# Batch 1's inputs laid out like batch 0's, and the head of an attention–MoE kernel in another order

## The chip, the cores and the metric

The kernel runs on one core of a Trainium2 chip. The metric is the device time of one execution in microseconds. The kernel before takes 725.71 us, the median of three runs (725.63 to 726.22).

## What is computed

Two batched attentions between tokens `x` and a small state share one score matrix. Their outputs, joined along the sequence, run through two mixture layers of the same shape, each a dense pair of matrices around a nonlinearity.

```python
# x: B, H, S, D = 4, 8, 512, 64; state: 4, 8, 32, 64
scores = x @ state.T / sqrt(D);  a  = softmax(scores);  xread = a  @ state
scores2 = state @ x.T / sqrt(D); a2 = softmax(scores2); sread = a2 @ x
x = concat([xread, sread], axis=2)         # 4*544 = 2176 rows of 512 after the transpose
h = x @ w_in                               # 512 -> 2048
g = where(h >= 1, h, where(h <= -1, 0, (h + 1)**2 / 4))
x = g @ w_out                              # 2048 -> 512
h = x @ w_in2; g = max(h, 0) + log1p(exp(-abs(h))); out = g @ w_out2
```

## The kernel before, in words

**Numbers.** Inputs come as 64-bit words and are read as pairs of 32-bit words. A weight tile is rebuilt by three steps of the class `Pair`: `scale` (ScalarE, L124) on the high words, `tail` (VectorE, L143) shifts the low words, and `join` (VectorE, L146) puts the two together. Products that need full accuracy are made of three, from a high part `hi` (ScalarE copy, L85) and a low part `lo` (VectorE subtraction, L88) of each factor: high by high, high by low, low by high (L623 to L625, L683).

**First layer without the read.** For a batch, `G = state · W_in` is computed once per pair of column tiles (`g_mm` by `heads`, L287), so the first layer of its tokens is the softmax weights `a` times `G`: six products at L683 for each hidden tile. A hidden tile goes through its activation (L772, L773 on ScalarE, L788 on VectorE), is cut into `gth` (ScalarE, L85) and `gtl` (VectorE, L88), and enters the second layer (L623 to L625).

**Order.** All is written out by hand: the kernel runs in `tc.manual_schedule()`, so each engine's queue holds its instructions in program order. A head (from `st0 = load_state0(...)` on) prepares batch 0; then a loop over windows runs. Window `i` carries the steps that a list of `ORDER` names: `l1` (first layer of this window's tile), `l2` (second layer of an earlier one), `hi`, `lo`, `open`, `close` (cuts and activations), `early`, `conv`, `split`, `load` (weights), `pe`, `copy` (other work). `when(i, kind, fn)` hangs work on a window. `HW` and `TW` hold windows for attention steps, and `HW[0]` that of `place_state`, which turns the state of all batches (TensorE L274, VectorE copy L275).

**The head.** `load_state0` brings the state of batch 0, 64 partitions, on ScalarE's queue; `load_x(0)` brings `x` of batch 0 in two loads of 1 KB runs on SyncE's queue, and `load_x(1)` that of batch 1 in four loads of 256-byte runs, behind the loads of the first weight pair. `warm` issues dummy products of the identity (L219). `x_transpose` turns `x` (L320 for batch 0, L316 for batch 1), `x_copy` moves the result to SBUF (ScalarE L85, the fourth VectorE L327); `place_state0` turns the state (TensorE L235, VectorE L236 into `stT0`). `scores_n` (L249) makes 64 narrow score products, `f_sub` and `f_exp` start the softmax, `scores0` (L261) makes the scores of the other side. `f_norm` sums, inverts and multiplies one half of the weights, with VectorE and GpSimd sharing it (L531 to L534); `f_turn` (L540) turns them for `n_hi` and `n_lo`, which cut them into `ahi` and `alo`. `x_turn` and `x_keep` turn `x` of batch 1 and keep it. Banks of PSUM are named `at` (with two halves `side`), `l1`, and `acc0` to `acc3`.

Of the kernel before, what the change touches and what calls it, by code (L numbers as in the profile page):

```python
# [18 lines left out]
def fused_kernel(ctx: ExitStack, tc: tile.TileContext, x, state, w1, w2, w3, w4, out):  # L19
# [79 lines left out]
    class Pair:  # L99
# [41 lines left out]

        def tail(self, d, raw):
            nc.vector.tensor_scalar(d, raw[:, 0::2], 29, None, op0=ALU.logical_shift_right)  # L143
# [28 lines left out]

    ident = new(p1, [P, P], F32, "ident")
    make_identity(nc, ident)
    stT = new(p1, [P, NJ, B * N], F32, "stT")
    stT0 = new(p1, [P, H * N], F32, "stT0")
# [3 lines left out]

    xt = {}

    def load_x(b, engs):
# [3 lines left out]
        if b == 0:  # L187
# [33 lines left out]
    def load_state0(eng):  # L221

        st = new(base, [P, 1024], F32, "cv", 2)[: H * N // 4]
        eng.dma_start(st[:, : 4 * D], state[0].rearrange("h (m i) d -> (h m) (i d)", i=4))
        return st

    def place_state0(st):

        n = H * N // 4
        one = st[:, : 4 * D].rearrange("p (i d) -> p i d", i=4)  # L230
        two = st[:, 512:].rearrange("p (i q d) -> p i q d", i=4, q=2)
        nc.vector.tensor_copy(two, one.unsqueeze(2).to_broadcast([n, 4, 2, D]))
        ps = at_bank()[:, : H * N]
        for i in range(4):
            nc.tensor.transpose(ps[:, i * n : (i + 1) * n], two[:, i].rearrange("p q d -> p (q d)"), ident[:n, :n])  # L235
        nc.vector.tensor_copy(stT0.rearrange("p (m i) -> p m i", i=4), ps.rearrange("p (i m) -> p m i", i=4))  # L236

    def scores_n(xT, js, out):


        for j in js:
            for e in range(2):
                for i in range(2):
                    for q in range(2):
# [5 lines left out]
                            out[q][:, o : o + N], xT[j][rows, c : c + P], stT0[rows, h * N : (h + 1) * N], start=True, stop=True  # L250
                        )

    def scores0(xT):

        for j in range(NJ):
            for e in range(2):
                for q in range(2):
# [4 lines left out]
                        side[j * N : (j + 1) * N, q, c], stT0[rows, h * N : (h + 1) * N], xT[j][rows, c], start=True, stop=True  # L262
# [14 lines left out]
    def heads(b, o, rhs):  # L277


        for j in range(NJ):  # L280
            for e in range(2):
                rows = slice(e * D, (e + 1) * D)
                if b == 0:
                    s_h = stT0[rows, (2 * j + e) * N : (2 * j + e + 1) * N]
                else:
                    s_h = stT[rows, j, b * N : (b + 1) * N]
# [15 lines left out]
    class Attn:  # L302
# [10 lines left out]
        def x_transpose(self, j, ps, r):  # L313
            xb, c = xt[self.b], slice(r * P, (r + 1) * P)
            if self.b > 0:
# [13 lines left out]
        def scores(self):  # L329

            if self.b == 0:
                scores0(self.xT)
            else:
                heads(self.b, lambda e: side[:, e, :], lambda j: self.xT[j])
            if self.b == 0:
                self.ps.update((g, side.rearrange("p q (e i t) -> p e q i t", e=2, i=2)[:, g]) for g in range(NG))
            else:
                self.ps.update((g, side[:, g, :]) for g in range(NG))
# [5 lines left out]
        def turned(self, t):  # L344

            return t.rearrange("p (i q t) -> p q i t", i=2, q=2) if self.b == 0 else t
# [114 lines left out]
        def x_turn(self):  # L461
            for j in range(NJ):
# [4 lines left out]
        def x_keep(self, i):  # L467

            t = new(p1, [P, NG, S], F32, ("ahi", "alo")[i])
            for e in range(2):  # L470
                j = 2 * i + e
                self.xT[j] = t[:, e, :]
                copy(self.xT[j], self.ps["x", j])
# [53 lines left out]
        def f_norm(self, J, eng):  # L527
            h = self.f_half(self.f, J)
            sm = new(at, [P, 2 * NB], F32, "sm", 2)[:, :NB]
            sm3 = sm.rearrange("p (c j) -> p c j", j=2)  # L530
            nc.vector.tensor_reduce(sm3, h, axis=AX.X, op=ALU.add)  # L531
            nc.vector.tensor_scalar(sm, sm, 1e-9, None, op0=ALU.add)
            nc.vector.reciprocal(sm, sm)
            eng.tensor_tensor(h, h, sm3.unsqueeze(3).to_broadcast([P, NB // 2, 2, N]), op=ALU.mult)  # L534
# [293 lines left out]
    HW = [5, 0, 6, 15, 17]  # L828
# [23 lines left out]
    for n, (a, pair) in enumerate(pairs):  # L852
# [73 lines left out]
    when(1, "pe", lambda: warm(W_[2]))  # L926
    when(1, "copy", lambda: [a0.s_copy(g) for g in range(NG)])
# [27 lines left out]
    with tc.manual_schedule():  # L955
# [11 lines left out]
        for J in range(2):  # L967
# [3 lines left out]
            if J == 0:  # L971
                place_state0(st0)
# [105 lines left out]
```

## Time and profile before

| what | value |
|---|---|
| median of 3 runs | 725.71 us (725.63 to 726.22) |
| the profiled execution's own time | 727.52 us |
| its span | 725.7 us |
| TensorE busy | 713.9 us (98%), 4038 instructions |
| VectorE busy | 443.1 us (61%) |
| ScalarE busy | 444.0 us (61%) |
| GpSimd busy | 17.9 us (2%) |
| mean granted clock of TensorE | 0.995 |

The span reaches from the first to the last instruction of one profiled execution; 1.8 us of that execution lie outside it, and it took 1.8 us more than the median run. Busy shares are means over stages with different limits, so a row of a stage counts for more than these. All times below are microseconds from the span's start.

### The profile page before, as it was taken

How to read it: one execution, taken by the hardware profiler on the slowest of the kernel's cores; microseconds unless marked ns; L12 is line 12 of the kernel's file. 1: busy time of each engine (PE TensorE's matmuls, PEld its weight loads, DVE VectorE, ACT ScalarE, POOL GpSimd, SP SyncE). 2: the span in 40 equal slices, each digit the busy share in tenths (PEclk: the TensorE clock that was granted, in tenths of full speed). 3: DMA queues.
4: the chain of work that ended last, by engine and by line, in shares of the span. 5: the costliest groups of instructions: out<-in, count | busy, mean ns of one | idle time of the engine just before them, and what ended most of it. 6: DMA issues, size and time to landing. Idle time of an engine off the chain costs nothing.

```text
span 725.7 us, 10250 instructions
## 1 busy us (share of the span) xinstructions
PE 713.9 (98%) x4038; PEld 577.9 (80%) x4038; DVE 443.1 (61%) x699; ACT 444.0 (61%) x730; POOL 17.9 (2%) x22
## 2 busy tenths in 40 slices
PE   8899999999999999999999999999999999999997
PEld 7667777777777887778888888888888888888886
DVE  5789975574684245767798756544555545544543
ACT  4787775555654356677887766555566556565553
POOL 0001200021000000000000000000000000000000
PEclk8999999999999999999999999999999999999999
DMA  9993005326150013353443011020002100010001
GB/s 264 387 291 120 0 1 118 60 64 112 59 172 4 1 62 114 131 172 118 146 145 131 22 38 59 11 63 0 1 0 79 39 0 1 1 58 1 1 0 58
DMA packets 61951, 56.29 MB, mean 78 GB/s; under 512 B 40976, under 2 KB 42832, under 8 KB 61904
## 3 DMA queue, kind: packets, MB, share of 16 engines
q1 hardware_dynamic: 61680, 55.46, 24.3%
q8 instruction: 31, 0.51, 0.3%
q10 hardware_dynamic: 224, 0.20, 0.1%
q14 instruction: 16, 0.13, 0.1%
HBM read 45.68 MB, written 9.96 MB: 77 GB/s over the span
## 4 chain that ended last, share of the span: by engine, by line
PE 89%; DMA 3%; DVE 3%; ACT 2%; SPq 2%; issue 1%; DVEq 0%; ACTq 0%
PE acc L623 16%; PE acc L624 16%; PE acc L625 16%; PE l L683 10%; PE l L624 9%; PE l L625 9%; PE l L623 9%; PE at L287 2%; PE l L670 2%; DMA wq<-in_moe_w_out_dram 1%; SPq L196 1%; DMA wq<-in_moe_w_in_dram 1%; DMA xs<-in_state_dram 1%; DVE cv L146 1%; PE at L413 1%
## 5 line engine op out<-in xcount | busy, mean ns | idle before, releaser
L88 DVE TENSOR_TENSOR gtl<-tl,gth 128x512 fp32r<-128x512 f32 x64 | 44.3, 692 | 144.1 <-ACT gth L85 143.9
L781 ACT ACTIVATE ta<-l 128x512 f32<-128x512 f32 x68 | 40.7, 598 | 132.3 <-PE l L625 132.3
L624 PE MATMUL acc<-gtl,wq 128*128 128x512 f32 x256 | 100.1, 391 | 2.0 <-DVE gtl L88 2.0
L623 PE MATMUL acc<-gth,wq 128*128 128x512 f32 x256 | 101.2, 395 | 0.6 <-ACT gth L85 0.6
L625 PE MATMUL acc<-gth,wq 128*128 128x512 f32 x256 | 99.7, 390 | 0.0
L88 DVE TENSOR_TENSOR gtl<-ta,gth 128x512 fp32r<-128x512 f32 x68 | 47.3, 696 | 67.1 <-ACT gth L85 67.1
L772 ACT ACTIVATE ta<-l 128x512 f32<-128x512 f32 x68 | 40.3, 593 | 47.3 <-PE l L683 31.1
L623 PE MATMUL acc<-wq,gth 128*128 128x512 f32 x152 | 59.2, 390 | 0.0
L624 PE MATMUL acc<-wq,gth 128*128 128x512 f32 x152 | 59.2, 389 | 0.0
L625 PE MATMUL acc<-wq,gtl 128*128 128x512 f32 x152 | 59.2, 389 | 0.0
L623 PEld LDWEIGHTS acc<-gth,wq 128*128 128x128 f32 x256 | 48.0, 188 | 13.3 <-issue 1.7
L624 PEld LDWEIGHTS acc<-gtl,wq 128*128 128x128 f32 x256 | 48.1, 188 | 12.8 <-DVE gtl L88 3.2
L625 PEld LDWEIGHTS acc<-gth,wq 128*128 128x128 f32 x256 | 48.1, 188 | 10.2
L623 PE MATMUL acc<-wh,gth 128*128 128x512 f32 x136 | 52.9, 389 | 0.0
L624 PE MATMUL acc<-wl,gth 128*128 128x512 f32 x136 | 52.9, 389 | 0.0
L625 PE MATMUL acc<-wh,gtl 128*128 128x512 f32 x136 | 52.9, 389 | 0.0
L88 DVE TENSOR_TENSOR tl<-tl,ta 128x512 f32<-128x512 f32 x68 | 47.0, 692 | 2.4
L788 DVE SCALAR_TENSOR_TENSOR ta<-ta,l 128x512 f32<-128x512 f32 x68 | 46.2, 679 | 0.5 <-ACT ta L773 0.5
L791 DVE SCALAR_TENSOR_TENSOR tl<-l,tl 128x512 f32<-128x512 f32 x68 | 46.5, 684 | 0.0
L792 DVE SCALAR_TENSOR_TENSOR ta<-tb,ta 128x512 f32<-128x512 f32 x68 | 46.4, 682 | 0.0
L85 ACT ACTIVATE gth<-ta 128x512 fp32r<-128x512 f32 x68 | 42.1, 619 | 6.8 <-DVE ta L788 6.8
L784 ACT ACTIVATE tl<-tb 128x512 f32<-128x512 f32 x68 | 43.0, 633 | 2.2
(189 smaller groups left out, 1475.5 us busy)
## 6 DMA issues: line engine op xcount, KB each, us to landing
ws<-in_moe_w_in_dram SPq DMA_DIRECT2D x20, 512.0 KB, 4.7
ws<-in_moe_w_out_dram SPq DMA_DIRECT2D x20, 512.0 KB, 4.1
wq<-in_moe_w_in_dram SPq DMA_DIRECT2D x12, 512.0 KB, 7.1
wq<-in_moe_w_out_dram SPq DMA_DIRECT2D x12, 512.0 KB, 8.8
xd<-xs SPq DMA_DIRECT2D x16, 256.0 KB, 3.0
xs<-xd SPq DMA_DIRECT2D x16, 256.0 KB, 3.9
out_dram<-xs SPq DMA_DIRECT2D x15, 256.0 KB, 2.3
x<-in_x_dram SPq DMA_DIRECT2D x12, 256.0 KB, 4.8
```

What stands on the lines that cost most here:

```text
L85: nc.scalar.activation(dst, src, AF.Copy)
L88: eng.tensor_tensor(dst, a, b, op=ALU.subtract)
L623: nc.tensor.matmul(o, lh, rh, start=first, stop=False)
L624: nc.tensor.matmul(o, lh, rl, start=False, stop=False)
L625: nc.tensor.matmul(o, ll, rh, start=False, stop=last)
L683: nc.tensor.matmul(w.h, l[:, g, f], r[:, g, :], start=i == 0, stop=i == len(terms) - 1)
L772: nc.scalar.activation(w.a, w.hc, AF.Relu, bias=1.0)
L781: nc.scalar.activation(w.a, w.hc, AF.Abs)
L784: nc.scalar.activation(w.l, w.b, AF.Ln)
L788: nc.vector.scalar_tensor_tensor(w.a, w.a, 1.0, w.hc, op0=ALU.min, op1=ALU.max)
L791: nc.vector.scalar_tensor_tensor(w.l, w.hc, 0.0, w.l, op0=ALU.max, op1=ALU.add)
L792: nc.vector.scalar_tensor_tensor(w.a, w.b, 1.0, w.a, op0=ALU.subtract, op1=ALU.subtract)
```

## The change

1. **State.** `load_state0` and `place_state0` take batches 0 and 1 at once: 128 partitions, transposes of 128 columns, and two VectorE copies `keep(0)`, `keep(1)` into `stT0[:, b]`. `keep(1)` is issued behind the last `x_copy`.
2. **x of batch 1** (`FAST = (0, 1)`) is loaded in two loads of 1 KB runs, as batch 0's; its scores are made by `scores0`.
3. **Low words.** For the first weight pair, ScalarE does the shift (`tail_act`, in bytes, with a bias tile `off`); VectorE keeps the join.
4. **Softmax of batch 0.** `f_sums` sums both halves, then one addition and one reciprocal; `f_norm(g)` multiplies by groups, group 0 on VectorE, group 1 on GpSimd. They stand ahead of the first product, which is followed by the turns of the weights.
5. **TensorE's head.** Seven dummy products behind `scores_n`; half of `x_turn` ahead of the first product and half behind it; `x_keep` by single tiles, the fourth behind `n_hi`.
6. **Window 1** gets a step `turn` with `a0.scores()`, which left the head, and two dummies in place of four.
7. **`HW[0]`** goes from 5 to 7: `place_state` two windows later.

```diff
-    W_ = (7, 4, 4)
+    W_ = (7, 7, 2, 4)
...
-        "l1 close split hi open scale lo conv copy early load pe".split(),
+        "l1 turn close split hi open scale lo conv copy early load pe".split(),
...
+        def tail_act(self, part):
+
+            d, raw = self.parts(part)
+            nc.scalar.activation(d, raw.bitcast(mybir.dt.uint8)[:, 3::8], AF.Identity, scale=1.0 / 32, bias=off)
...
+    FAST = (0, 1)
...
+    nc.gpsimd.memset(off, 1.0 / 64 - 0.5)
...
-        if b == 0:
+        if b in FAST:
             t = t.rearrange("p (h r d) -> p h r d", h=H, r=R)
...
-        eng.dma_start(st[:, : 4 * D], state[0].rearrange("h (m i) d -> (h m) (i d)", i=4))
+        st = new(base, [P, 1024], F32, "cv", 2)
+        eng.dma_start(st[:, : 4 * D], state[: len(FAST)].rearrange("b h (m i) d -> (b h m) (i d)", i=4))
...
+            nc.tensor.transpose(ps[:, i * P : (i + 1) * P], two[:, i].rearrange("p q d -> p (q d)"), ident)
+
+        def keep(b):
+            src = ps.rearrange("p (i b m) -> p b m i", i=4, b=len(FAST))[:, b]
+            nc.vector.tensor_copy(stT0[:, b].rearrange("p (m i) -> p m i", i=4), src)
...
+        def f_sums(self):
+            self.sm = new(at, [P, 2 * NB], F32, "sm", 2)
+            for J in range(2):
+                dst = self.sm.rearrange("p (c j) -> p c j", j=NJ)[:, :, 2 * J : 2 * J + 2]
+                nc.vector.tensor_reduce(dst, self.f_half(self.f, J), axis=AX.X, op=ALU.add)
+            nc.vector.tensor_scalar(self.sm, self.sm, 1e-9, None, op0=ALU.add)
+            nc.vector.reciprocal(self.sm, self.sm)
+
+        def f_norm(self, g, eng):
+            h = self.f.rearrange("p (c g j n) -> p c g j n", g=NG, j=NJ, n=N)[:, :, g]
+            sm = self.sm.rearrange("p (c g j) -> p c g j", g=NG, j=NJ)[:, :, g]
+            eng.tensor_tensor(h, h, sm.unsqueeze(3).to_broadcast([P, NB // 4, NJ, N]), op=ALU.mult)
...
-    HW = [5, 0, 6, 15, 17]
+    HW = [7, 0, 6, 15, 17]
...
-                when(a, f"conv{i}", lambda pair=pair, i=i: pair.conv(i, 2))
+                when(a, f"early{i}", lambda pair=pair, i=i: pair.tail_act(i))
+                when(a, f"conv{i}", lambda pair=pair, i=i: pair.join(*pair.parts(i)))
...
+    when(1, "turn", lambda: a0.scores())
...
             if J == 0:
-                place_state0(st0)
+                keep = place_state0(st0)
+                keep(0)
             for j in (2 * J, 2 * J + 1):
                 a0.x_copy(j, ps[j], j != 3)
+        keep(1)
         run(-3, "early0")
         run(-3, "early1")
-        run(-3, "conv0")
         halves_n = ([side[:, q, :] for q in range(2)], [bank("l1", 2) for q in range(2)])
         for J in range(2):
             scores_n(a0.xT, (2 * J, 2 * J + 1), halves_n[J])
+        warm(W_[1])
         a0.f_sub(0, halves_n[0])
         a0.f_exp(0)
-        run(-3, "conv1")
+        run(-3, "conv0")
         a0.f_sub(1, halves_n[1])
         a0.f_exp(1)
+        run(-3, "conv1")
+        a0.f_sums()
+        a0.f_norm(0, nc.vector)
+        a0.f_norm(1, nc.gpsimd)
+        a1 = attn(1)
+        a1.x_turn((0, 1))
         two = [bank(f"acc{2 + g}", 1) for g in range(NG)]
         g_mm(0, 0, two)
+        a1.x_keep(0)
         hi, lo = g_tiles(0, 0)
         for g in range(NG):
             copy(hi[:, g, :], two[g][:, :C2])
-        a0.scores()
-        a1 = attn(1)
-        a1.x_turn()
-        for i in range(2):
-            a1.x_keep(i)
-        warm(W_[1], bank("acc0", 1))
-        a0.f_norm(0, nc.gpsimd)
-        a0.f_norm(1, nc.vector)
+        a1.x_turn((2, 3))
+        a1.x_keep(1)
+        a1.x_keep(2)
+        warm(W_[3], side[:, 0, :])
         for g in range(NG):
             a0.f_turn(g, bank(f"acc{g}", 1))
             a0.n_hi(g)
+        a1.x_keep(3)
         run(-1, "early")
```

TensorE's queue in the head, before, from the end of the first product (`w1_0`, the first weights, and `stT0`, the state) to the turns of the softmax weights (`cv_31`). L261 is the scores of the other side, L316 the turns of batch 1, L219 dummies.

```order
L287 MATMUL acc2_41_224<-w1_0_36_173,stT0_4_76 32x256
L287 MATMUL acc3_42_225<-w1_0_36_173,stT0_4_76 32x256
L261 MATMUL at_1_69<-xT0_32_155,stT0_4_76 32x256 x4
L261 MATMUL at_1_69<-xT1_33_157,stT0_4_76 32x256 x4
L261 MATMUL at_1_69<-xT2_34_167,stT0_4_76 32x256 x4
L261 MATMUL at_1_69<-xT3_35_169,stT0_4_76 32x256 x4
L316 MATMUL acc0_45_254<-ident_2_70,x1_14_94 128x128 x4
L316 MATMUL acc1_46_259<-ident_2_70,x1_14_94 128x128 x4
L316 MATMUL l1_47_264<-ident_2_70,x1_14_94 128x128 x4
L316 MATMUL l1_48_269<-ident_2_70,x1_14_94 128x128 x4
L219 MATMUL acc0_51_280<-ident_2_70 128x128 x4
L540 MATMUL acc0_54_295<-ident_2_70,cv_31_140 128x128 x4
```

The same engine in the change, from behind the score products of batch 0 (lines are now 234 for dummies, 339 for turns of `x`, 306 for the first product):

```order
L234 MATMUL acc3_40_211<-ident_2_70 128x128 x7
L339 MATMUL acc0_44_240<-ident_2_70,x1_15_96 128x128 x4
L339 MATMUL acc1_45_245<-ident_2_70,x1_15_96 128x128 x4
L306 MATMUL acc2_46_250<-w1_0_37_173,stT0_4_76 32x256
L306 MATMUL acc3_47_251<-w1_0_37_173,stT0_4_76 32x256
```

and from the end of the first product to the first hidden tile (L561 turns the softmax weights, L704 is its product):

```order
L306 MATMUL acc2_46_250<-w1_0_37_173,stT0_4_76 32x256
L306 MATMUL acc3_47_251<-w1_0_37_173,stT0_4_76 32x256
L339 MATMUL l1_51_266<-ident_2_70,x1_15_96 128x128 x4
L339 MATMUL l1_52_271<-ident_2_70,x1_15_96 128x128 x4
L234 MATMUL at_1_69<-ident_2_70 128x128 x4
L561 MATMUL acc0_54_283<-ident_2_70,cv_32_140 128x128 x4
L561 MATMUL acc1_55_289<-ident_2_70,cv_32_140 128x128 x4
L704 MATMUL l1_58_309<-ahi_26_134,gh_49_262 128x512 x2
```

The other side's scores are gone from here, and half of the turns stand ahead of the first product behind seven dummies. The scores stand now behind the first two hidden tiles, in window 1, ahead of two dummies and the first second-layer product (L644):

```order
L704 MATMUL l1_60_319<-alo_27_135,gh_49_262 128x512 x2
L280 MATMUL at_1_69<-xT0_33_155,stT0_4_76 32x256 x4
L280 MATMUL at_1_69<-xT1_34_157,stT0_4_76 32x256 x4
L280 MATMUL at_1_69<-xT2_35_167,stT0_4_76 32x256 x4
L280 MATMUL at_1_69<-xT3_36_169,stT0_4_76 32x256 x4
L234 MATMUL acc3_68_362<-ident_2_70 128x128 x2
L644 MATMUL acc0_69_365<-gth_62_346,wq0_61_343 128x512
```

VectorE's queue in the head, before, from the state copy on (`w1_0` is rebuilt by L143 and L146, `mx` are the row maxima of the scores in `at`):

```order
L236 COPY stT0_4_76<-at_1_69 128x256
L327 COPY xT3_35_169<-acc3_30_139 128x512
L143 TENSOR_SCALAR w1_0_36_173<-wq0_13_91 128x512
L146 SCALAR_TENSOR_TENSOR w1_0_36_173<-wq0_13_91,w1_0_36_173 128x512
L520 TENSOR_REDUCE mx_39_210<-at_1_69 128x8
L88 TENSOR_TENSOR cv_31_140<-at_1_69,mx_39_210 128x4x64
L520 TENSOR_REDUCE mx_39_210<-at_1_69 128x8
L88 TENSOR_TENSOR cv_31_140<-at_1_69,mx_39_210 128x4x64
```

and in the change (L253 are the state copies, L346 is `x_copy(3)`, L158 the join):

```order
L253 COPY stT0_4_76<-at_1_69 128x256
L346 COPY xT3_36_169<-acc3_31_139 128x512
L253 COPY stT0_4_76<-at_1_69 128x256
L537 TENSOR_REDUCE mx_41_219<-at_1_69 128x8
L88 TENSOR_TENSOR cv_32_140<-at_1_69,mx_41_219 128x4x64
L537 TENSOR_REDUCE mx_41_219<-at_1_69 128x8
L88 TENSOR_TENSOR cv_32_140<-at_1_69,mx_41_219 128x4x64
L158 SCALAR_TENSOR_TENSOR w1_0_37_173<-wq0_14_93,w1_0_37_173 128x512
```

The second state copy stands behind the copy of `xT3` and ahead of the maxima; the shift is gone and the first join stands behind the first two maxima.

ScalarE's queue, before, around the copies of the turned softmax weights (`ahi_25`) and the second weight pair's conversion (`wq1_15`):

```order
L85 ACTIVATE alo_50_277<-l1_47_264 128x512
L85 ACTIVATE alo_50_277<-l1_48_269 128x512
L85 ACTIVATE ahi_25_134<-acc0_54_295 128x512
L85 ACTIVATE ahi_25_134<-acc1_55_301 128x512
L124 ACTIVATE wq1_15_99<-wq1_15_99 128x1024
```

and in the change (the copies of the turned weights go to `ahi_26`, those of batch 1's `x` to `alo_53`):

```order
L85 ACTIVATE alo_53_277<-l1_51_266 128x512
L85 ACTIVATE ahi_26_134<-acc0_54_283 128x512
L85 ACTIVATE ahi_26_134<-acc1_55_289 128x512
L85 ACTIVATE alo_53_277<-l1_52_271 128x512
L124 ACTIVATE wq1_16_99<-wq1_16_99 128x1024
```

The fourth copy of batch 1's `x` moved from ahead of the copies of the turned weights to behind them, ahead of the conversion.

## Rows read from the trace of the kernel before

**Rows 1.** Busy time by stage: stretch, its length, each engine's busy time, granted clock, DMA.
```profile
24.00:45.00 21.00, 18.78 (x120) 12.62 (x118) 17.31 (x22) 16.98 (x25) 0.00 (x0) 1.00 1.05 359
...
70.00:725.70 655.70, 650.64 (x3593) 530.39 (x3591) 388.94 (x620) 395.98 (x659) 14.70 (x14) 1.00 0.19 56
```

**Rows 2.** Timeline of TensorE at 71 us: start, duration, line, tiles, count, idle before.
```profile
71.14 0.50 PE L624 MATMUL acc<-gtl,wq 128*128 128x512 f32 x1 [0.44 <-DVE gtl L88]
```

**Rows 3.** TensorE's waits, 24 to 75 us: total, times, longest.
```profile
PE acc L624 <- DVE gtl L88: 2.0, 3, 0.8
PE at L287 <- DVE stT L275: 0.8, 1, 0.8
```

**Rows 4.** Timeline of TensorE: start, time until the last ends, line, tiles, count.
```profile
1.35 3.36 PE L219 MATMUL acc<-ident 128*128 128x128 f32 x14 [1.35 <-POOL ident masks.py:199]
4.50 1.19 PE L320 MATMUL acc<-ident,x 128*128 128x128 f32 x8
...
7.16 1.98 PE L249 MATMUL at<-stT,xT 64*128 64x32 f32 x32
8.97 1.96 PE L249 MATMUL l<-stT,xT 64*128 64x32 f32 x32
10.85 0.64 PE L287 MATMUL acc<-w,stT 64*32 64x256 f32 x8
12.66 0.65 PE L287 MATMUL acc<-w,stT 64*32 64x256 f32 x4 [1.18 <-DVE w L146]
...
13.12 2.55 PE L261 MATMUL at<-xT,stT 64*32 64x256 f32 x28
15.60 1.97 PE L316 MATMUL acc<-ident,x 128*128 128x128 f32 x8
17.36 1.57 PE L316 MATMUL l<-ident,x 128*128 128x128 f32 x8
...
19.93 1.06 PE L540 MATMUL acc<-ident,cv 128*128 128x128 f32 x8
21.25 0.99 PE L683 MATMUL l<-ahi,gh 128*128 128x512 f32 x2 [0.25 <-ACT ahi L85]
...
27.33 0.50 PE L624 MATMUL acc<-gtl,wq 128*128 128x512 f32 x1 [0.84 <-DVE gtl L88]
```

**Rows 5.** Timeline of ScalarE, 20 to 25 us.
```profile
20.60 1.09 ACT L85 ACTIVATE ahi<-acc 128x512 fp32r<-128x512 f32 x2 [1.03 <-PE acc L540]
21.57 1.13 ACT L124 ACTIVATE wq<-wq 128x1024 f32<-128x1024 f32 x1
...
24.37 1.04 ACT L85 ACTIVATE wq<-cv 128x1024 fp32r<-128x1024 f32 x1
```

**Rows 6.** Timeline of VectorE, 6 to 28 us.
```profile
6.11 0.42 DVE L236 COPY stT<-at 128x256 f32<-128x256 f32 x1 [0.96 <-PE at L235]
7.27 0.69 DVE L327 COPY xT<-acc 128x512 f32<-128x512 f32 x1 [0.73 <-PE acc L320]
...
14.82 0.17 DVE L532 TENSOR_SCALAR sm<-sm 128x16 f32<-128x16 f32 x1
...
15.86 0.65 DVE L532 TENSOR_SCALAR sm<-sm 128x16 f32<-128x16 f32 x1
...
22.73 1.23 DVE L146 SCALAR_TENSOR_TENSOR cv<-wq,cv 128x1024 uint32<-128x1024 uint32 x1 [0.21 <-ACT wq L124]
...
26.59 0.69 DVE L88 TENSOR_TENSOR gtl<-ta,gth 128x512 fp32r<-128x512 f32 x1
```

**Rows 7.** Windows of one microsecond, with the granted clock (the number before the DMA share).
```profile
11.00:12.00 1.00, 0.49 (x8) 0.01 (x1) 0.86 (x4) 0.49 (x1) 0.00 (x0) 0.81 1.17 217
...
17.00:18.00 1.00, 1.00 (x6) 1.00 (x5) 1.00 (x3) 0.75 (x2) 0.00 (x0) 0.50 0.84 297
18.00:19.00 1.00, 1.00 (x9) 1.00 (x9) 0.20 (x1) 0.75 (x3) 0.00 (x0) 0.78 0.95 305
```

**Rows 8.** Timeline of GpSimd, 14 to 17 us.
```profile
15.44 1.05 POOL L534 TENSOR_TENSOR cv<-cv,sm 128x512 f32<-128x512 f32 x1 [14.14 <-ACT gh L85]
```

More of the change, by code (lines that the diff above doesn't have):

```diff
@@ L140, in rebuild, with parts @@
             self.join(d, raw)
+        def parts(self, part):
+            if self.v is None:
+                self.v = new(p1, [P, NK, C2], F32, f"w1_{self.p}")
+                self.dst[self.p] = self.v
+            d = flat(self.v).bitcast(U32)[:, part * 512 : (part + 1) * 512]
+            return d, self.raw[:, part * 512 * M : (part + 1) * 512 * M]
+        def tail_act(self, part):
+            d, raw = self.parts(part)
+            nc.scalar.activation(d, raw.bitcast(mybir.dt.uint8)[:, 3::8], AF.Identity, scale=1.0 / 32, bias=off)
         def tail(self, d, raw):
@@ L175, in fused_kernel @@
     stT = new(p1, [P, NJ, B * N], F32, "stT")
-    stT0 = new(p1, [P, H * N], F32, "stT0")
+    stT0 = new(p1, [P, len(FAST), H * N], F32, "stT0")
     x1s = new(p1, [P, NJ, B * N], F32, "x1s")
@@ L179, in fused_kernel @@
     xds = new(dram, [P, NK, P], F32, "xds")
+    off = new(base, [P, 1], F32, "off")
+    nc.gpsimd.memset(off, 1.0 / 64 - 0.5)
     xt = {}
@@ L249, in scores_n, with scores0 @@
                         nc.tensor.matmul(
-                            out[q][:, o : o + N], xT[j][rows, c : c + P], stT0[rows, h * N : (h + 1) * N], start=True, stop=True
+                            out[q][:, o : o + N], xT[j][rows, c : c + P], stT0[rows, 0, h * N : (h + 1) * N], start=True, stop=True
                         )
-    def scores0(xT):
+    def scores0(b, xT):
         for j in range(NJ):
@@ L261, in scores0 @@
                     nc.tensor.matmul(
-                        side[j * N : (j + 1) * N, q, c], stT0[rows, h * N : (h + 1) * N], xT[j][rows, c], start=True, stop=True
+                        side[j * N : (j + 1) * N, q, c], stT0[rows, b, h * N : (h + 1) * N], xT[j][rows, c], start=True, stop=True
                     )
@@ L282, in heads @@
                 rows = slice(e * D, (e + 1) * D)
-                if b == 0:
-                    s_h = stT0[rows, (2 * j + e) * N : (2 * j + e + 1) * N]
+                if b in FAST:
+                    s_h = stT0[rows, b, (2 * j + e) * N : (2 * j + e + 1) * N]
                 else:
@@ L314, in x_transpose @@
             xb, c = xt[self.b], slice(r * P, (r + 1) * P)
-            if self.b > 0:
+            if self.b not in FAST:
                 nc.tensor.transpose(ps[:, c], xb[:, r, 2 * j : 2 * j + 2, :].rearrange("p e d -> p (e d)"), ident)
@@ L329, in scores @@
         def scores(self):
-            if self.b == 0:
-                scores0(self.xT)
+            if self.b in FAST:
+                scores0(self.b, self.xT)
+                self.ps.update((g, side.rearrange("p q (e i t) -> p e q i t", e=2, i=2)[:, g]) for g in range(NG))
             else:
                 heads(self.b, lambda e: side[:, e, :], lambda j: self.xT[j])
-            if self.b == 0:
-                self.ps.update((g, side.rearrange("p q (e i t) -> p e q i t", e=2, i=2)[:, g]) for g in range(NG))
-            else:
                 self.ps.update((g, side[:, g, :]) for g in range(NG))
@@ L459, in x_block, with x_turn @@
                 nc.vector.transpose(self.xT[j], xy[self.b].pop(j))
-        def x_turn(self):
-            for j in range(NJ):
+        def x_turn(self, js):
+            for j in js:
                 self.ps["x", j] = bank(f"acc{j}", 1) if j < 2 else bank("l1", 2)
@@ L465, in x_turn, with x_keep @@
                     self.x_transpose(j, self.ps["x", j], r)
[L467 to L473, printed above, removed]
+        def x_keep(self, j):
+            i, e = divmod(j, 2)
+            if e == 0:
+                self.pair = new(p1, [P, NG, S], F32, ("ahi", "alo")[i])
+            self.xT[j] = self.pair[:, e, :]
+            copy(self.xT[j], self.ps["x", j])
         def head(self):
@@ L1042, in fused_kernel @@
                     cut_lo(v)
-                elif what in ("split", "early", "conv", "late", "pe", "load", "copy", "scale"):
+                elif what in ("split", "early", "conv", "late", "pe", "load", "copy", "scale", "turn"):
                     run(i, what)
```

19 lines of the change are left out of this document (4 added, 15 removed).

## The prediction

> **What bounds the kernel now.** I read the granted clock first: it is 0.995 over the span, so only a short stretch can run slow. Then the busy time by stage: behind 70 us TensorE works 650.64 of 655.70 us, while from 24 to 45 us VectorE and ScalarE are about as busy as TensorE [rows 1]. Of the waits behind, the first is 0.44 us at 71.14, for the low half `gtl` of a hidden tile [rows 2]; in all 655.70 us TensorE is idle for 5.06, spread thin. So a gain of the head is kept if it is still there when the wait for `gtl` near 71 us ends: behind it no engine but TensorE sets the pace. Of the waits between 24 and 75 us, the three on `gtl` sum to 2.0 us and one on the state copy is 0.8 us [rows 3]. VectorE sets the shift there, so what counts is when VectorE's chain begins, and less what TensorE does between.
>
> The chain that starts it, read back from the first low product (27.33, after 0.84 us of idle) [rows 4]: `gtl` (26.59) stands on VectorE behind the low part of the first second-layer weights, which waits for ScalarE's cut `wq<-cv` (24.37); this stood on ScalarE behind the activations of the first hidden tile, whose six products began at 21.25 [rows 4 to 6]. They waited for ScalarE's copy of the turned softmax weights (20.60), which waited for the turns at 19.93. The same cut also needs VectorE's join at 22.73, which waits for ScalarE's conversion at 21.57 [rows 5, 6]. Both branches meet at the cut, and both hang on the turns.
>
> And the turns are late because of the clock. It was 0.81 of full in 11–12 us, 0.50 in 17–18, 0.78 in 18–19, and full again from 19 [rows 7]: the lower level, 1.2 GHz, for nearly 7 us. TensorE had run 64 narrow score products (32 columns each) and then went idle before the fall; before the rise it had worked without pause from 12.66. The start of the span shows the lower level too: 14 rows of dummies in 3.36 us, and the transposes behind them at the upper level (8 in 1.19 us, against 1.97 for 8 of the same shape at 15.60) [rows 4].
>
> **The change part by part.** *State of two batches at once.* The scores of batch 0 now wait for the second half copy `keep(1)`, since that copy stands behind `x_copy(3)` on VectorE and reads the same PSUM bank that the scores write. By rows: `x_copy(3)` runs 7.27 to 7.96, then 0.42 as the present copy of the same shape, so the first score starts at about 8.35 in place of 7.16 [rows 4, 6]: +1.2 us, with TensorE idle for 1.1 of it. Behind this wait stands everything on TensorE; the row maxima on VectorE and the exponentials on ScalarE wait for the scores. The doubled state load and the wider broadcast have no row: twice the packets lie between 0 (the scores wait for `keep(1)`, not for the state) and +0.1; transposes of 128 in place of 64 columns between 0 and +0.2. I take 0, as the bank is next needed only behind `x_copy(3)`.
>
> *Scores.* They take 7.16 to 10.92 now, 3.77 us, mostly at the upper level [rows 4]; from 8.35, with a fall at 11.6 as before, the last 0.5 us takes twice as long: end near 12.5.
>
> *Seven new dummies.* At the lower level the seven at the start took 3.36 us, about 3.0 without the filling of the pipeline [rows 4]: 12.4 to 15.4. They lie beside work: the joins of the first weights are due on VectorE near 12.7 and 14.9, so the first product could not run earlier by more than half a microsecond.
>
> *Order behind.* Turns of batch 1, tiles 0 and 1: 8 rows, 1.76 us at the lower level (15.60 to 17.36), so 0.88 at the upper one [rows 4]; the first product, 16 rows, 0.7 as I take it (8 rows took 0.64 with the filling at 10.85); turns 2 and 3 0.88; four dummies about 0.9 (half of what four sevenths of 3.36 is). 15.4 + 3.4 = 18.8. The first four turns of softmax weights are done 0.6 later, ScalarE's copy takes 0.6, and the first hidden product starts at about 20.0 in place of 21.25: −1.2. What makes this possible is that the sums and both normalisations now precede the first product, and that the scores of the other side (2.55 us at the lower level, at 13.12 now) [rows 4] have left the head. They come back in window 1 at about half that, in TensorE's wait for `gtl`, of which 1.3 us was filled with four dummies or idle; two dummies leave.
>
> *ScalarE and VectorE to the low product.* Copies 19.4 to 20.5; `x_keep(3)`, now ahead of the conversion, 0.5; conversion 20.9 to 22.0 (21.57 before, −0.7); join to 23.3; meanwhile the two activations end by 23.3; the cut at 23.3 in place of 24.37. The same steps as now behind it give `gtl` done at 26.2, the low product at 26.25: **−1.1**.
>
> *ScalarE shifts low words.* Removed: two shifts on VectorE of 0.43. Added: two passes on ScalarE, of which no row exists: 0.68 as the conversion of the same shape on ScalarE, or twice that for its strided bytes. Even 1.4 each ends before the joins' place in VectorE's queue, between the maxima. Price 0, upper end +0.3.
>
> *x of batch 1 in 1 KB runs.* The turns at 15.60 have no idle in front [rows 4], so no one waits for these loads; they are also the first on TensorE to need them. 0. Two loads fewer on the SyncE queue pull the weights behind them forward; nothing waited for these from 19 us on. Scores of batch 1 become 32x256 products: about +0.5 of TensorE near 50 us.
>
> *State of batches 2 and 3 two windows later.* The 0.8 us wait goes [rows 3]; the same copy delays VectorE as much later, still before 71 us. TensorE's gain and the +0.5 go into the wait for `gtl` there (0.4 left). 0.
>
> **Sum.** 727.52 (the profiled execution) − 1.1 = 726.4; the median of the runs shown lies 1.8 lower, so 725.71 − 1.1 = **724.6**. Ends of this case: 723.9 if the level returns while the dummies run (0.7 earlier), 725.2 with +0.3, +0.2 and +0.1 of the unknowns. About a measurement's reach from no change is 0.2%, 1.45 us: faster is under 724.26, slower above 727.16.
>
> **One pair of rows beside a rule.** VectorE's addition of 128x16 took 0.17 at 14.82 and 0.65 at 15.86, while GpSimd multiplied (15.44 to 16.49) [rows 6, 8]. In the change the two halves of the normalisation become ready together at about 16.6, on VectorE (0.69, as the copy of as many elements at 7.27) and GpSimd (1.05): side by side they end at 17.66, one after the other at 18.35. The turns come at 18.8 in my case, so 724.6 holds by both; only where the turns are early (C below) it is 723.3 or 723.8. The Trainium skill, "SBUF — State Buffer", section "Who interferes with whom", says that a VectorE instruction with two SBUF inputs and a GpSimd instruction that reads SBUF exclude each other, the second blocking fully; by that rule they go one after the other. The trace agrees for the addition, for two multiplications no row here shows it.
>
> **The rivals.** *A, forecast:* the level falls near 11.6 and the dummies do what those at the start did. For it: the same narrow scores and no pause from 8.35 on. 0.54.
> *B, the dummies do not bring it back:* the lower level lasts to 18.4 as now. Then turns end at 17.2, product 18.5, turns 19.4, dummies 20.3, copy 21.5: +0.3, **726.0**. For it: in the middle of the present span the rise came only after 5.8 us of work [rows 4, 7]. 0.24.
> *C, the level never falls, or briefly:* no pause follows the scores. Scores end at 12.1, dummies 13.7, and the product waits for the second join (14.9); the turns wait for the normalisation at 17.66; first hidden product at 18.9: −2.4, **723.3**. Against it: the fall came as the narrow products had only just ended. 0.12.
> *D, slower:* the new pause of TensorE at 7.23 to 8.35 brings the fall forward. Place: the first score row. Each microsecond that the fall comes before 11.6 makes the scores end one later; at 10.5 the gain is gone, before 9.0 it is slower by over 0.2%. From 8.35 on: scores to 15.9, dummies to 18.9, the rest as in A, first hidden product at 23.5: +2.2, **727.9**. For it: in the present trace, too, a pause and the lower level stand side by side (11.49 and 11.6). Against it: pauses of 0.25 to 0.84 us later in the head cost no clock [rows 4]. 0.10.
> *The 1 KB runs do shorten the load stream,* but nothing waits for it; this is inside A.
>
> **How the numbers follow.** The forecast is A's 724.6. Faster: C, and a third of A (its part under 724.26): 0.12 + 0.17 = 0.29. Slower: D, 0.10. Same: the rest, 0.61. The range leaves out D and the outer edges of B and C: 723.2 to 726.6. A's own is 723.9 to 725.2.
>
> **What would show it.** In the profile after: about 1.1 us of TensorE idle before the first score with VectorE's state copy as releaser; scores 8.4 to 12.5; clock low at 12–15 only; the first hidden product at 20.0; the first low product at 26.3; no 0.8 us wait at the scores of batch 1; a wait for `gtl` still near 70. Wrong would be: a clock below 0.9 before 11 us or after 16, `gtl` no longer the last wait near 70, or a join that waits for ScalarE's shift.

## The result and the profile after

The change takes **734.31 us** (733.05 to 737.28, 6 runs) where the kernel before takes 725.78 (725.51 to 727.31, 6 runs): ratio **1.0123**, 95% interval 1.0098 to 1.0148. It is slower by 8.5 us; 1.1 less was forecast. The profiled execution took 733.05, its span is 731.2.

The head went nearly as forecast. TensorE's timeline after, with the columns of [rows 4] (L339 turns of `x`, L268 scores, L234 dummies, L561 turns of the softmax weights, L704 first hidden tile, L645 first low product):

```profile
1.35 3.36 PE L234 MATMUL acc<-ident 128*128 128x128 f32 x14 [1.35 <-POOL ident masks.py:199]
5.00 1.19 PE L339 MATMUL acc<-ident,x 128*128 128x128 f32 x8 [0.29 <-DMA x<-in_x_dram]
...
8.78 1.97 PE L268 MATMUL at<-stT,xT 64*128 64x32 f32 x32 [1.21 <-DVE stT L253]
10.56 2.29 PE L268 MATMUL l<-stT,xT 64*128 64x32 f32 x32
12.78 3.10 PE L234 MATMUL acc<-ident 128*128 128x128 f32 x14
15.72 1.04 PE L339 MATMUL acc<-ident,x 128*128 128x128 f32 x8
...
19.11 1.04 PE L561 MATMUL acc<-ident,cv 128*128 128x128 f32 x8
20.39 0.99 PE L704 MATMUL l<-ahi,gh 128*128 128x512 f32 x2 [0.25 <-ACT ahi L85]
...
26.61 0.50 PE L645 MATMUL acc<-gtl,wq 128*128 128x512 f32 x1 [0.84 <-DVE gtl L88]
```

TensorE waits 1.21 us for VectorE's state copy, the scores run 8.8 to 12.9, the dummies 12.8 to 15.7. The windows after show the lower clock level where case A had put it (compare [rows 7]):

```profile
12.00:13.00 1.00, 1.00 (x11) 0.94 (x10) 0.97 (x4) 0.50 (x1) 0.00 (x0) 0.54 1.04 410
13.00:15.00 2.00, 2.00 (x10) 2.00 (x11) 1.93 (x6) 0.45 (x2) 0.00 (x0) 0.50 1.02 394
15.00:16.00 1.00, 1.00 (x9) 1.00 (x8) 1.00 (x3) 0.31 (x1) 0.00 (x0) 0.76 1.03 383
16.00:20.00 4.00, 4.00 (x47) 3.32 (x45) 3.03 (x7) 2.49 (x6) 1.48 (x1) 1.00 1.06 391
```

The first low product starts at 26.61 in place of 27.33. From there to the end of the span the kernel before needs 725.7 − 27.33 = 698.4 us, the change 731.2 − 26.61 = **704.6**. No wait accounts for these 6.2 us. TensorE's waits after, 24 to 75 us and then 70 to the end:

```profile
PE acc L645 <- DVE gtl L88: 1.6, 3, 0.8
PE at L306 <- ACT xT L85: 0.8, 1, 0.8
```

```profile
PE at L430 <- DVE gl L88: 0.5, 1, 0.5
PE acc L645 <- DVE gtl L88: 0.4, 1, 0.4
```

What differs is the pace of the products. One window of 100 us in which TensorE is busy throughout at full clock, of the kernel before and of the change (the number behind x is the products begun):

```profile
500.00:600.00 100.00, 100.00 (x443) 82.81 (x442) 50.26 (x79) 59.14 (x100) 0.00 (x0) 1.00 0.07 22
```

```profile
500.00:600.00 100.00, 100.00 (x438) 81.84 (x437) 50.90 (x81) 57.37 (x96) 0.00 (x0) 1.00 0.07 22
```

443 products against 438. By groups of instructions between 300 and 700 us (busy time, mean ns of one), before and after:

```profile
L623 PE MATMUL acc<-wq,gth 128*128 128x512 f32 x128 | 49.8, 389 | 0.0
...
L623 PE MATMUL l<-x,wq 128*128 128x512 f32 x88 | 34.2, 389 | 0.0
```

```profile
L644 PE MATMUL acc<-wq,gth 128*128 128x512 f32 x128 | 50.0, 391 | 0.0
...
L644 PE MATMUL l<-x,wq 128*128 128x512 f32 x88 | 34.8, 396 | 0.0
```

The products of the tokens `x` with the weights are 7 ns slower each, those of `wq` with `gth` 2 ns, with no other operand and no other order. What the change did move is where tiles lie. Its bias tile `off` is 4 bytes per partition and takes 32; it lies first in the pool `base`, so all tiles behind it in this pool and in the pools above (weights, `gth`, `gtl`, four of the six `wh` and of the six `wl`) moved by 32 bytes. The state tile `stT0` grew too, by 1 KB, but that moves the tiles behind it by a multiple of 512 bytes, which will turn out not to matter. The pool with the second layer's tokens is laid out from the other end of the memory and stayed.

### The profile page after: what moved, and what is told of

Read it like the earlier page. It is cut to its first block, busy times and chain, and to the rows that moved or that the text cites. A ratio compares the mean times of both kernels' runs of the same rounds, so it can differ in the third digit from the quotient of the medians.

```text
span 731.2 us, 10299 instructions
## 1 busy us (share of the span) xinstructions
PE 720.4 (99%) x4064; PEld 578.8 (79%) x4064; DVE 441.8 (60%) x696; ACT 445.0 (61%) x732; POOL 18.4 (3%) x23
## 4 chain that ended last, share of the span: by engine, by line
PE 91%; ACT 4%; DVE 3%; issue 1%; DMA 1%; DVEq 0%; ACTq 0%
PE acc L644 16%; PE acc L645 16%; PE acc L646 16%; PE l L704 10%; PE l L644 9%; PE l L645 9%; PE l L646 9%; PE at L306 2%; PE l L691 2%; DVE cv L158 1%; DMA x<-in_x_dram 1%; PE at L430 1%; ACT gh L85 1%; ACT gth L85 0%; ACT ta L794 0%
## 5 line engine op out<-in xcount | busy, mean ns | idle before, releaser
L645 PE MATMUL acc<-gtl,wq 128*128 128x512 f32 x256 | 100.2, 392 | 1.6 <-DVE gtl L88 1.6
L644 PE MATMUL acc<-gth,wq 128*128 128x512 f32 x256 | 101.4, 396 | 0.0
L644 PE MATMUL acc<-wq,gth 128*128 128x512 f32 x152 | 59.5, 391 | 0.0
L645 PE MATMUL acc<-wq,gth 128*128 128x512 f32 x152 | 59.4, 391 | 0.0
L645 PEld LDWEIGHTS acc<-gtl,wq 128*128 128x128 f32 x256 | 48.1, 188 | 12.5 <-DVE gtl L88 2.7
L644 PEld LDWEIGHTS acc<-gth,wq 128*128 128x128 f32 x256 | 48.1, 188 | 12.5 <-issue 2.1
L645 PE MATMUL acc<-wl,gth 128*128 128x512 f32 x136 | 53.3, 392 | 0.0
L644 PE MATMUL acc<-wh,gth 128*128 128x512 f32 x136 | 53.3, 392 | 0.0
L803 ACT ACTIVATE ta<-ta 128x512 f32<-128x512 f32 x68 | 43.1, 634 | 2.2
```

Source lines behind the costliest of these rows:

```text
L644: nc.tensor.matmul(o, lh, rh, start=first, stop=False)
L645: nc.tensor.matmul(o, lh, rl, start=False, stop=False)
L803: nc.scalar.activation(w.a, w.a, AF.Exp, scale=-1.0)
```

## The experiments

**Theory P**: a 512-column product is late when its moving tile and the weights that are loaded for the next product start at different places within some power of two of bytes: 64 in the first trial, then 128, then 512. I counted pairs of neighbouring products that are unlike in this sense in the built programs. A product is called late when the next one starts 229 ns or more behind its own start. **Rival C**: the loss comes with the head's new order or its clock. All runs (unlike: long pairs that differ within 512 bytes; clock: mean granted from 7 to 27 us; low: start of the first low product; rest: span less this; these three from the profiled execution):

| kernel | unlike | clock | low | rest | median, us | ratio to before, interval |
|---|---|---|---|---|---|---|
| before | 37 | 0.83 | 27.33 | 698.4 | 725.78 | |
| before_again | 37 | 1.00 | 25.52 | 698.4 | 726.30 | 1.0000 (0.9985–1.0016) |
| change | 863 | 0.91 | 26.61 | 704.6 | 734.31 | 1.0123 (1.0098–1.0148) |
| off_64 | 863 | 0.91 | 26.98 | 704.3 | 734.11 | 1.0112 (1.0091–1.0132) |
| off_128 | 855 | 0.83 | 30.17 | 703.5 | 734.13 | 1.0111 (1.0096–1.0126) |
| **off_512** | 24 | 0.91 | 26.80 | **698.3** | 728.48 | 1.0029 (1.0014–1.0043) |
| before_off_4 | 874 | 0.91 | 25.44 | **705.0** | 732.26 | 1.0098 (1.0064–1.0132) |
| before_pad_96 | 681 | 0.91 | 26.42 | 703.9 | 731.64 | 1.0073 (1.0058–1.0088) |
| pad_96 | 863 | 0.83 | 28.82 | 704.3 | 734.29 | 1.0106 (1.0089–1.0123) |
| pad_112 | 863 | 0.83 | 28.84 | 703.8 | 735.06 | 1.0128 (1.0111–1.0145) |
| **pad_208** | 219 | 0.91 | 27.22 | **699.2** | 729.55 | 1.0041 (1.0021–1.0060) |
| off_128_no_dummies | 855 | 0.83 | 27.21 | 703.5 | 733.48 | 1.0105 (1.0090–1.0120) |
| off_128_keep_early | 855 | 0.91 | 26.07 | 703.5 | 732.02 | 1.0086 (1.0069–1.0103) |
| off_512_no_dummies | 24 | 0.83 | 27.15 | 698.2 | 727.35 | 1.0015 (0.9998–1.0032) |
| off_512_keep_early | 24 | 0.91 | 25.85 | 698.3 | 725.67 | 0.9999 (0.9983–1.0014) |
| keep_early_hw5 | 24 | 0.91 | 25.94 | 698.2 | 725.76 | 1.0000 (0.9982–1.0017) |
| keep_early_3 | 24 | 0.91 | 27.26 | 698.1 | **725.14** | 0.9991 (0.9976–1.0005) |
| keep_early_0 | 24 | 0.91 | 27.07 | 698.1 | 725.47 | 0.9993 (0.9977–1.0008) |
| before_state_128 | 37 | 0.83 | 28.91 | 698.4 | 726.72 | 1.0004 (0.9980–1.0027) |
| keep_early_3_state_sp | 24 | 0.91 | 25.78 | 698.2 | 727.48 | 1.0019 (0.9999–1.0038) |

### Where the tiles lie

off_64, then off_128, then off_512 change only the room of the bias tile:

```diff
-    off = new(base, [P, 1], F32, "off")
+    off = new(base, [P, 16], F32, "off")[:, :1]    # off_128: 32, off_512: 128
```

> The change with its 4-byte bias tile given 64 bytes of each partition in place of 32, so that every tile behind it starts at a multiple of 64 bytes again; nothing else differs. Theory P (a 512-column product starts about 7 ns late when the moving tile and the next weights lie at different places within 64 bytes; 854 such pairs in the change, 0 in the kernel before): all pairs alike, 226.7 ns from start to start, and the time falls by 6 to 7.5 us, to 726 to 728 at the clock levels the change ran with, 725.1 where the clock is as in its profile. Rival C (the loss comes with the head: clock, order or another engine's load): no change, 733 to 737.

Missed: 734.11, rest 704.3. Told apart by their tiles' starts, the pairs now differed by 64 bytes, and 99% of those with the tokens were late.

> The change with its bias tile given 128 bytes of each partition, so that every tile behind it keeps the place within 128 bytes that it has in the kernel before; nothing else differs. Theory P2 (a 512-column product is some 7 ns late when moving tile and next weights start at different places within 128 bytes; 854 such pairs in the change and with 64 bytes, 0 here): start to start 226.7 ns behind 200 us as before, about 6.5 us less than the change, and what is left is the head's gain of 0.7: 725.1, between 724.3 and 726.5 by the clock's level in the head. Rival C (order of the head or another engine's load): 733 to 735.

Missed too: 734.13, rest 703.5, with a difference of 128 bytes.

> The change with its bias tile given 512 bytes of each partition, so that the tiles behind it keep their place within 512 bytes (one row of a weights tile of 128 columns). Theory P3 (a 512-column product is 6 to 7 ns late when moving tile and next weights start at different places within 512 bytes; of the long products 863 such pairs in the change, 855 with 128 bytes, 37 in the kernel before, 24 here): start to start 226.7 ns behind 300 us as before, and only the head's gain of 0.7 is left: 725.3, between 724.5 and 727 by the clock's level in the head. Rival C (the order of the head or other work slows the products): 733 to 735 as with 64 and 128 bytes.

Met in the pace: rest 698.3, 6% of the pairs late as in the kernel before, and the window and the group of above are back:

```profile
500.00:600.00 100.00, 100.00 (x443) 82.84 (x442) 51.06 (x80) 58.40 (x98) 0.00 (x0) 1.00 0.06 22
```

```profile
L644 PE MATMUL l<-x,wq 128*128 128x512 f32 x88 | 34.3, 389 | 0.0
```

5.8 us of the 8.5 are gone (734.31 to 728.48). Not met in the total, where 725.3 was expected: 728.48 − 698.3 − 1.8 would put the low product at about 28.4 in the median execution, if the rest is the same there (one execution alone was profiled), see the head below. The other side of the test adds the tile alone to the kernel before:

```diff
+    off = new(base, [P, 1], F32, "off")
+    nc.gpsimd.memset(off, 1.0 / 64 - 0.5)
```

> The kernel before with the bias tile alone added (4 bytes, set by GpSimd, read by nobody), so that the tiles behind it move by 32 bytes and all else stays. Theory P: 854 unlike pairs at about 7 ns, +6.0, and about 1 more for pairs that both start in the middle of 64 bytes: 732 to 733. Rival C: 725.8, no change.

Met: 732.26, rest 705.0 against 698.4, and the window of the change is there:

```profile
500.00:600.00 100.00, 100.00 (x438) 81.86 (x437) 50.79 (x80) 57.80 (x97) 0.00 (x0) 1.00 0.07 22
```

**Together with off_512 this shows that 6 us come from the tile's place and not from anything in the head.** The third pair of tests moves the tokens' pool by its filler tile, in the kernel before and in the change:

```diff
-                nc.gpsimd.memset(new(pools["x"][0], [P, 88], F32, "pad"), 0.0)
+                nc.gpsimd.memset(new(pools["x"][0], [P, 96], F32, "pad"), 0.0)    # pad_112, pad_208: 112, 208
```

> The kernel before with the same filler at 96: its layer-2 tokens move to the middle of 64 bytes, the weights stay at multiples of 64, 644 unlike pairs. Theory P and P': +4.0 to +4.6, about 730, all of it behind 75 us and the first 75 us as before. Rival C: 725.8.

Slower as forecast, but by more: 731.64 and rest +5.5, where +4.0 to +4.6 was expected.

> The change with the filler tile of layer 2's pool at 96 elements in place of 88, so that this pool's tiles (the tokens that move through TensorE) start in the middle of 64 bytes too, like nearly all others: 210 unlike pairs in place of 854. Theory P, likeness decides: 644 pairs gain 5 to 7 ns, 3.2 to 4.5 us, so about 730 (from 734.3). Theory P', only a start at a multiple of 64 is fast: no gain or a loss, 734 or more. Rival C: no change.

> The change with the filler of layer 2's pool at 112 elements, so that this pool too starts 32 bytes behind a multiple of 128 bytes, like nearly all other tiles: 210 unlike pairs in place of 854, all of them ahead of 160 us. Theory P2, likeness decides: 644 pairs gain about 6.7 ns, 4.3 us, about 730. Theory P2', only starts at a multiple of 128 are fast: 734 or more. Rival C: no change, 734.

Both missed for the same reason as off_64: the pools were brought alike within 64 and within 128 bytes, and still differed by 64 and 128.

> The change with the filler of layer 2's pool at 208 elements, so that this pool lies 32 bytes off within 512 bytes too: 219 unlike long pairs in place of 863, absolute starts as odd as in the change. Theory P3, likeness decides: 644 pairs gain 6.5 ns, 4.2 us, about 730. Theory P3' (only the kernel before's own places are fast): no gain, 734. Rival C: 734.

Met: 729.55, rest 699.2, although nearly every tile starts 32 bytes off the places of the kernel before. Likeness decides, not the absolute start.

From start to start, behind 75 us, the 756 unlike pairs in the change's trace take 233.5 ns in the mean, and all of them 229 or more; like pairs of the kernel before take 227.0, and 6% of them 229 or more. In the change 22% of the like pairs are late as well. Most of these, 280 of 400, are among the first five like pairs behind a run of unlike ones, and further behind only 8% are late. So a run of unlike pairs also delays a few like ones after it; why these is open. An estimate from these means: 756 pairs at 6.5 ns are 4.9 us, and five pairs behind each of the 70 runs add about 1.4 us, together close to the 6.2 us.

Whether the next product's weights count, as theory P has it, or a product's own, is not settled, since nearly always both differ alike. Where only the next are unlike, all of 12 pairs are late at a difference of 32 bytes (change), none of 12 at 64 (off_64) and all of 12 at 128 (off_128). Where only the own are, it is none of 2, none of 2 and both.

### The head

> The kernel before, unchanged, for a second profile. Theory H (the first profile, 727.52, had the long low level, 6.8 us, which is not usual; the twin with the bias tile alone had 3.4 us and its first low product at 25.44): low level 3.4 us or less, first low product at 25.3 to 25.9, span 723.7 to 724.7, time 725.5 to 726.5. Rival: the first profile is typical, low product at 27.3, span 725.7.

Theory H met. TensorE's timeline of this second profile of the kernel before:

```profile
4.83 1.97 PE L320 MATMUL acc<-ident,x 128*128 128x128 f32 x8
...
8.22 1.98 PE L249 MATMUL at<-stT,xT 64*128 64x32 f32 x32
...
13.11 0.42 PE L287 MATMUL acc<-w,stT 64*32 64x256 f32 x4 [0.56 <-DVE w L146]
...
14.73 1.43 PE L316 MATMUL acc<-ident,x 128*128 128x128 f32 x8
...
19.43 1.00 PE L683 MATMUL l<-ahi,gh 128*128 128x512 f32 x2 [0.25 <-ACT ahi L85]
...
25.52 0.50 PE L624 MATMUL acc<-gtl,wq 128*128 128x512 f32 x1 [0.85 <-DVE gtl L88]
```

```profile
12.00:20.00 8.00, 6.89 (x82) 4.82 (x82) 7.48 (x17) 4.96 (x11) 1.05 (x1) 1.00 1.08 364
```

Once up, the level does not fall again in this head, and the turns of batch 1 take 1.43 us for 8 where [rows 4] have 1.97. It rose later, though: the first turns of `x` took 1.97 here, against 1.19 in [rows 4]. 25.52 + 698.4 + 1.8 outside the span = 725.7, the usual run; 27.33 was 1.8 us later, as the first profiled execution was longer (727.52). With a low level of half that length (before_off_4) it is 25.44. So against the usual head of the kernel before, off_512's 26.80 is **1.3 us behind**, not ahead.

> As off_512, with the second state copy right behind the first on VectorE. By theory K and the trace with 128 bytes (first score at 8.24 with x landing 0.8 later, low product at 26.07): low product at 25.6 to 26.1, 0.5 to 1 less than off_512, 724.3 to 724.8, faster than the kernel before. Rival: the clock's fall takes it back, as off_512.

```diff
                 keep(0)
+                keep(1)
             for j in (2 * J, 2 * J + 1):
                 a0.x_copy(j, ps[j], j != 3)
-        keep(1)
```

Theory K (the scores wait for the second state copy, and that costs TensorE's time) met in the head: the low product comes at 25.85, 0.95 earlier. The time, 725.67, is 2.8 less than off_512's, but 724.3 to 724.8 and faster than the kernel before was expected, and the two are not told apart. The scores no longer wait:

```profile
7.01 1.09 PE L339 MATMUL acc<-ident,x 128*128 128x128 f32 x8
8.03 1.98 PE L268 MATMUL at<-stT,xT 64*128 64x32 f32 x32
...
12.02 3.12 PE L234 MATMUL acc<-ident 128*128 128x128 f32 x14
```

In other executions the gain is larger than in this pair of profiles: the whole run's mean clock was under 0.997 in 10 of 11 executions of off_512 and in 2 of 12 of this kernel. This mean also counts the end of the span, where the level can fall (0.50 in the last microsecond of keep_early_hw5), so it only points to a longer low level in the head.

```diff
-    W_ = (7, 7, 2, 4)
+    W_ = (7, 0, 2, 4)    # keep_early_3, on the kernel with the early copy: (7, 3, 2, 4)
```

> As off_512, without the seven dummies. By theory D1 and the trace with 128 bytes (level back at 18.4 in place of 15.5, low product at 27.2): 0.6 slower than off_512, about 725.9, like the kernel before. Rival D2: 0.5 to 1.5 less than off_512.

Theory D1 is that the dummies bring the clock's level back, its rival D2 that they only delay. The level did as D1 says, the time as D2: the level was low for longer (0.83 against 0.91), and the low product came 0.35 later than off_512's; but the median is 1.1 less, 727.35. The two intervals overlap, so what the dummies cost or give over all executions is not settled; the profiles show only that the low level was shorter with them in this pair. With 128 bytes, the same step (733.48 against 734.13, where up to 0.9 more was expected by D1) and the early copy (732.02) have the same signs, again with intervals that overlap, and there the clock was 0.83 with the dummies and without.

> off_512_keep_early with three dummies behind the scores in place of seven. Theory E (three keep TensorE at work until the joins; the rest only delay): turns start at 13.4 in place of 15.0, low product at 25.0 to 25.5, about 0.5 less than off_512_keep_early, 725.2. Rival D1 (fewer dummies and the level stays low for 6.8 us): low product near 26.5, 0.7 more.

> off_512_keep_early without the dummies behind the scores. Theory D1: long low level as in both traces without dummies so far, low product at 26.2 (27.15 less 0.95), time 0.3 to 0.6 more than off_512_keep_early, 726.2. Theory E: short level, low product near 25, 725.0.

725.14, as theory E has it (725.2), and 725.47, between its 725.0 and D1's 726.2, against 725.67. Both profiles fell on executions in which TensorE's clock first rose only at about 10 us (low product at 27.1 to 27.3, times 727.2 and 727.0), so the medians say more: the intervals overlap, so how many dummies are best is not settled, but with three or none no loss is seen. keep_early_3 has the lowest median of all kernels here, 0.9 under the kernel before, but its interval reaches 1.0005.

```diff
-    HW = [7, 0, 6, 15, 17]
+    HW = [5, 0, 6, 15, 17]
```

> off_512_keep_early with the turn of the other batches' state back in the window where the kernel before has it. Forecast's step (worth 0, since VectorE sets the pace until 71 us): from the first low product to the end 698.2 as now; the wait of 0.8 on the state copy returns at the scores of batch 1 near 50, and the wait for gtl near 71 shrinks. Rival: from the low product to the end 698.6 to 699.0, time 0.4 to 0.8 more.

Forecast's step met: rest 698.2, against 698.3 with the later turn. The wait on the state copy is back in this kernel (first line), and without it another of the same size stood in its place, on the copies of batch 1's scores (second line, off_512_keep_early):

```profile
PE at L280 <- DVE stT L294: 0.9, 1, 0.9
```

```profile
PE at L306 <- ACT xT L85: 0.8, 1, 0.8
```

The last two move the state's load:

```diff
-        st = new(base, [P, 1024], F32, "cv", 2)[: H * N // 4]
-        eng.dma_start(st[:, : 4 * D], state[0].rearrange("h (m i) d -> (h m) (i d)", i=4))
+        full = new(base, [P, 1024], F32, "cv", 2)
+        st = full[: H * N // 4]
+        eng.dma_start(full[:, : 4 * D], state[:2].rearrange("b h (m i) d -> (b h m) (i d)", i=4))
```

> The kernel before with the state load of the change alone: 128 partitions, two batches, of which the second half is read by nobody. Theory S (the larger load delays the first half of x): first transpose of x at 5.2 to 5.6 with a wait for x in front, in place of 4.5 to 5.3; time up to 0.5 more than the kernel before, where the head's later steps don't absorb it. Rival: 4.5 to 5.0, the spread is between executions.

```diff
                 engs[i % len(engs)].dma_start(t[:, c], src[:, c])
+                if b == i == 0:
+                    first.append(load_state0(nc.sync))
...
-        st0 = load_state0(nc.scalar)
...
+        st0 = first[0]
```

> keep_early_3 with the state's load issued on SyncE's queue between the two halves of x, in place of ScalarE's queue ahead of them. Theory S: first transpose of x at 4.6 to 5.0, the state transposes not later than their place behind it (about 6), scores 0.3 to 0.6 earlier, time 0.2 to 0.5 less than keep_early_3 (724.6 to 724.9), a version faster than both kernels. Rival: the state lands later than 6 and the second half of x after 7, so the scores come as late or later, 725.1 to 725.6.

Theory S fits: the transposes of `x` wait for the load until 5.60 (first line). They start at 5.00 to 5.78 in the 15 profiles of kernels with the larger load ahead of `x`, and at 4.50 to 5.29 in the four without it. What this delay costs is not shown: the time (726.72) is not told apart from the kernel before. The remedy brought the first half of `x` forward, to 4.50, but failed as its rival said (lines behind the first): the second half came at 7.74, and the scores at 8.76, against 8.03 in off_512_keep_early. Its time, 727.48, lies above the rival's 725.1 to 725.6 too.

```profile
5.60 1.97 PE L321 MATMUL acc<-ident,x 128*128 128x128 f32 x8 [0.89 <-DMA x<-in_x_dram]
```

```profile
4.50 1.46 PE L342 MATMUL acc<-ident,x 128*128 128x128 f32 x8
...
7.74 1.09 PE L342 MATMUL acc<-ident,x 128*128 128x128 f32 x8 [1.34 <-DMA x<-in_x_dram]
8.76 1.98 PE L271 MATMUL at<-stT,xT 64*128 64x32 f32 x32
```

## Why the prediction was wrong

- **The step that failed most** is "ScalarE shifts low words: price 0, upper end +0.3". Its two passes were priced well: 0.73 and 0.75 us on ScalarE, no join waited for them. But the step brought a tile, and I priced no tile. Its place made about 830 more pairs of products unlike: 6.2 us behind 27 us. The step "a gain of the head is kept" was right (698.4 and 698.3 in before and off_512), and its ground, "no engine but TensorE sets the pace", was right too: TensorE itself became slower.
- **The base of the sum**, "727.52 − 1.1", compared case A with an execution in which the kernel before had the long low level. I carried the difference of 1.8 between that execution and the median along as a constant. It was the head itself (25.52 against 27.33). So the gain of 1.1 in the sum was not there: with the tile's place put right, the change is still slower (off_512, 728.48 against 726.05 for the kernel before beside it, ratio 1.0029). Nearly all signs that the prediction named came true, within 0.4 us, and the total missed even so, as none of them watched TensorE's pace behind 27 us.
- **The wait for `keep(1)`** was right in place and, in the profiles, in size: 1.21 us of idle, 0.95 at the low product. In the medians it was worth 2.8 (off_512 against off_512_keep_early). Scores started at 8.78, 0.4 later than forecast, since the first half of `x` came 0.5 late (5.00 against 4.50); the doubled state load, priced 0 to 0.1, is the likely cause by the two groups of starts above.
- **The dummies**: the level came back at 15.5 as in case A here, but not in each execution (pad_96, pad_112 and off_128 have clock 0.83 with the same seven). A and B were both right, each in some executions.
- **Rival D** did not occur: no profile shows the level falling in the new pause. It had the right sign for a wrong reason.
- **The later state turn, the 1 KB runs and the moved scores** were worth 0, as forecast: rest is 698.2 or 698.3 with the turn in either window, and the turns at 15.72 have no idle in front.
- **The contention of VectorE and GpSimd** showed where it was put. Both multiplications, 17.07 and 17.19:

```profile
17.07 0.69 DVE L555 TENSOR_TENSOR cv<-cv,sm 128x512 f32<-128x512 f32 x1
```

```profile
17.19 1.48 POOL L555 TENSOR_TENSOR cv<-cv,sm 128x512 f32<-128x512 f32 x1 [15.89 <-DVE sm L550]
```

GpSimd's took 1.48 where 1.05 is its time alone [rows 8], VectorE's 0.69 as alone: the second to start took 0.43 us longer. The Trainium skill, "SBUF — State Buffer", section "Who interferes with whom", calls the contention an exclusive lock on a shared port pair. The trace points the same way, if not in full: they ran side by side from 17.19 to 17.76, 0.57 us, so a wait for the whole of it would be 0.57. The addition that the prediction set beside that rule has one SBUF input and not the two that it names; [rows 6, 8] show that it ended with GpSimd's multiplication (16.51 and 16.49). The delay was hidden: the turns at 19.11 have no idle in front.

## What to carry to other kernels

A new tile, however small, moves all tiles behind it in its pool and in the pools above. Where TensorE is the bound, compare the places of moving tiles and weights before and after a change, and give a small tile the room that keeps them (here 512 bytes); to put it last would do the same by this account, but was not tried. And before a sum is made against one profiled execution, see whether its own time is the usual one: where it is off by as much as the forecast gain, profile the kernel before a second time.

## What was not expected of the hardware

- A product of 512 columns starts 227.0 ns after the one before, or about 233.5, by how the moving tile and the weights lie to each other within 512 bytes of a partition. Differences of 32, 64 and 128 bytes are late in the mean (233.5 in the change, 233.1 in off_64, 232.7 in off_128), a multiple of 512 is not; 256 was not tried. At 64 bytes some kinds of pairs are not late, and which resource of the memory is shared is open. The Trainium skill, "SBUF — State Buffer", section "Who interferes with whom", gives TensorE two read ports, for the moving operand and for the weights, and calls them independent; here the two are not independent in time, since their places cost 6 us in 700.
- TensorE's granted clock falls once in the head in 19 of the 20 profiles here, at 11.3 to 13.8 us, and stays at the lower level for 3.4 or for 6.8 us, with the same instructions too (3.4 in the change, 6.8 in pad_96). In the second profile of the kernel before it did not fall in the head at all.
